# Inverting the triangular blocks of a delta-rule kernel on lanes of 16x16 instead of 32x32, in all twelve groups

## The chip, the cores and the metric

The kernel runs on one core of one Trainium2 chip. The time is the device time of one execution in microseconds. Before the change it is 664.31 us, the median of 3 runs (662.4 to 664.77).

## The reference

Two layers follow each other. The first is a delta-rule attention over 4 batches, 8 heads, 768 positions and a head size of 48; the second is a gated MLP on its output.

```python
k_n = k / (np.linalg.norm(k, axis=-1, keepdims=True) + 1e-06)
for t in range(S):
    y[:, :, t] = np.einsum('bhd,bhde->bhe', q[:, :, t], state)
    v_old = np.einsum('bhde,bhd->bhe', state, kt)
    state = state + bt * np.einsum('bhd,bhe->bhde', kt, vt - v_old)
# x: y with the heads side by side, (4, 768, 384)
h = np.maximum(x @ w_in, 0.0)                 # 1024 wide
u, v = h[..., :512], h[..., 512:]
v_n = (v - mean(v)) / sqrt(var(v) + 1e-06)    # over the 512
v_s = einsum('ts,bsd->btd', w_spatial, v_n) + b_spatial[None, :, None]
out = (u * v_s) @ w_out
```

## The kernel before

**The recurrence in chunks.** Each batch's 768 positions are cut into 12 chunks of 64 (`CH`). One *step* handles one chunk of one batch for all 8 heads: 4 pairs of heads (`NU`) in the free dimension, and the two heads of a pair on partitions 0 to 63 and 64 to 127. There are 48 steps. `ORDER` runs them as two chains of two batches each: six steps of the first chain alone, then one of each chain in turn, and six of the second chain alone.

Within a chunk the recurrence needs the inverse of a triangular 64x64 matrix per head, made of products of the keys (`products`, which multiplies on TensorE at line 359 and masks the results into the tile `ta` on VectorE). Four steps form a *group* (`G = 4`), and there are 12 groups; the blocks of a group are inverted together.

**Lanes.** The small triangular blocks on the diagonal are inverted by substitution on VectorE, each partition (a *lane*) working on its own block, so that one instruction handles all blocks of a group. To spread the blocks over lanes, `bounce` (line 399) writes the group's products to a buffer in DRAM, and loads pick the blocks out of it.

- Groups 1 to 11 use lanes of 32x32: `load_la` loads the block's rows in two parts with eight DMAs (line 512), `load_wt` and `load_wb` copy them into a work tile on ScalarE (lines 522 and 529), and `lanes` does 30 rounds of a multiply (line 543) and an add (line 550) on VectorE. A group has 64 such blocks; each is split over two lanes, its even rows on one and its odd rows on the other. The result goes to DRAM (`wd`, line 559, two DMAs) and comes back into `ta` (line 564, four DMAs).
- Group 0 uses lanes of 16x16, one block to a lane, 128 blocks: `load16` takes four DMAs (line 422), `copy16` one ScalarE copy, and `lanes16` does 14 rounds (lines 441 and 448). The inverted 16x16 blocks are stored (four DMAs, line 453), and `ta` is read back whole (line 458). Then two blocks of 16 are widened to one of 32 on TensorE: per step one VectorE transpose (line 465), 16 products (line 474), one ScalarE copy that masks half the rows (line 481), 16 more products (line 487) and four ScalarE copies into `ta` (line 493). `C16` is the number of steps that share one PSUM tile of the pool `pa`, one mask copy and one set of four copies; it is 1. On the chip one such product in 32-bit floats is two matmul instructions.

Both ways end with blocks of 32. The widening from 32 to 64 is part of every step: `step_t` transposes on VectorE (line 575), `step_e` and `step_f` multiply on TensorE (585, 597) and copy on ScalarE (588, 600). A step then has `step_a` (642, with an add on VectorE at 645), `step_b` (659, scaled at 663), `step_c` (678, added to the state at 682) and `step_d` (692, copied out at 703). All of these take their PSUM tiles from the pool `pa`, four banks in turn.

**The MLP.** When four chunks of a batch are done, `convert` splits the result into two parts for exact products, and tasks are put in a list: `mlp_v` (line 759), `mlp_u` (820), `mlp_g` (839) and `mlp_o` (884). They are TensorE work between the recurrence's pieces: `fill(rate)` emits a given amount of it after each part of a step, and what is left follows after the last step. The weights come in 64-bit floats and are decoded by short VectorE and ScalarE operations (line 156 and 183) in the first third.

**The order.** The prologue (all up to the loop over steps) sets VectorE's order by hand: group 0's lanes, with pieces of group 1's lanes (`X1 = 14` of them, and `M4` later) and of the weights' conversion between. In the loop a planner orders every engine's instructions by a simulated time and by priority: the parts of a step have a higher one (`hp`), products, lanes and MLP have that of their place. The lanes of group g+2 begin to be emitted in the third step of group g (`if sl == LS`), a few pieces at a time (`lane(n)` advances the oldest generator in `lq` by n pieces); before the fourth step of group g ends, the code makes sure that group g+1's lanes are emitted. `W16 = 16` is a number of empty pieces between the store of the 16x16 blocks and the first transpose, for groups other than 0. All loads and stores are issued by SP, in order.

The few lines that choose between the two ways:

```python
if g + 2 < G16:
    load16(g + 2)
    copy16(g + 2)
    lq.append(lanes16(g + 2))
else:
    load_la(g + 2)
    load_wt(g + 2)
    lq.append(lanes(g + 2))
```

Of the kernel before, what the change touches and what calls it, by code (L numbers as in the profile page):

```python
# [7 lines left out]
F32 = mybir.dt.float32  # L8
# [11 lines left out]
G = 4  # L20
# [8 lines left out]
R0 = 1.5  # L29
TD = 1  # L30
TP = 4
G16 = 1
C16 = 1
W16 = 16
X1 = 14
R1 = 1.7
# [42 lines left out]
def delta_rule_gated_mlp(  # L79
# [14 lines left out]
    nc = tc.nc  # L94
    PSUM = bass.MemoryType.PSUM
    const = ctx.enter_context(tc.tile_pool(name="const", bufs=1))
    grp = ctx.enter_context(tc.tile_pool(name="grp", bufs=2))
# [144 lines left out]
    def pump1():  # L242
        n = count["dve"]
        for _ in range(3 * len(tasks)):
            if not tasks or count["dve"] > n:
                break
            t = tasks.pop(0)
            if t[1] > 0:
                t[1] -= 1
            else:  # L250
                try:
                    t[1] = next(t[0])
                except StopIteration:
                    continue
            tasks.append(t)
# [139 lines left out]
    def bounce(g):  # L395
        ad_g[g] = dram.tile([CH, 2, G * NU, CH], F32, name="ad")
        ta = ta_g[g][:, 0].rearrange("p s u t -> p (s u) t")
        for h in range(2):
            mark["ad"] = nc.sync.dma_start(out=ad_g[g][:, h], in_=ta[rows_t(h)])

    ws = [const.tile([128, 16, 32], F32, name=f"w{i}") for i in range(2)]
    for w in ws:
        nc.gpsimd.memset(w[:, 8:16, 0:16], 0.0)

    def lane_map(g, blk):
        p0, r0 = blk * 32, blk * 16
        src = ad_g[g].rearrange("j h n t -> (h n) j t")
        return slice(p0, p0 + 32), src[:, r0 : r0 + 16, r0 : r0 + 16]

    buf16 = {}  # L410

    def load16(g):
        if g < 2:
            t = moe.tile([128, 512], F32, name="la16", tag="vl", bufs=VB)
        else:
            t = grp.tile([128, 16, 32], F32, name="la", bufs=1).rearrange("p j t -> p (j t)")
        buf16[g] = t
        la = t[:, 0:256].rearrange("p (j t) -> p j t", t=16)
        w = t[:, 256:512].rearrange("p (j t) -> p j t", t=16)
        for blk in range(4):  # L420
            pr, sq = lane_map(g, blk)
            mark["la"] = nc.sync.dma_start(out=la[pr], in_=sq)
        w_g[g] = [la, w]
# [5 lines left out]
    def lanes16(g):  # L429
        la, w = w_g[g]  # L430
# [29 lines left out]
        for _ in range(W16 if g else 0):  # L460
            yield
        pp = px = None
        for s in range(G):
            tr = buf16[g][:, s % 2 * 256 : s % 2 * 256 + 256].rearrange("p (u t) -> p u t", t=CH)
            t_ins = nc.vector.transpose(out=tr.rearrange("p u t -> p (u t)"), in_=ta[:, s].rearrange("p u t -> p (u t)"))
            yield
            if s % C16 == 0:
                pp = pa.tile([128, 512], F32, name="pa")
                px = pp[:, 256:512].rearrange("p (s u t) -> p s u t", u=NU, t=16)
                pp = pp[:, 0:256].rearrange("p (s u t) -> p s u t", u=NU, t=16)  # L470
            for u in range(NU):
                for q in range(4):
                    r, c = q * 32, q % 2 * 32
                    nc.tensor.matmul(
                        pp[r : r + 32, s, u], ta[r : r + 16, s, u, c : c + 32], tr[r : r + 16, u, c : c + 16],
                        start=True, stop=True,
                    )
            if s % C16 < C16 - 1:
                continue
            ss = slice(s - C16 + 1, s + 1)  # L480
            nc.scalar.mul(out=pi[:, ss], in_=pp[:, ss], mul=hm)
            yield
            for z in range(s - C16 + 1, s + 1):
                for u in range(NU):
                    for q in range(4):
                        r, c = q * 32, q % 2 * 32
                        p_ins = nc.tensor.matmul(
                            px[r : r + 16, z, u], pi[r : r + 32, z, u], ta[r : r + 32, z, u, c + 16 : c + 32],
                            start=True, stop=True,
                        )  # L490
            for q in range(4):
                r, c = q * 32, q % 2 * 32
                nc.scalar.copy(out=ta[r : r + 16, ss, :, c + 16 : c + 32], in_=px[r : r + 16, ss])
            if s == C16 - 1:
                mark["t16"], mark["p16"] = t_ins, p_ins
            yield s
# [76 lines left out]
    def step_t(s):  # L573
        tn_t[s] = work.tile([128, NU, 32], F32, name="tn", bufs=1)
        nc.vector.transpose(out=tn_t[s], in_=t_of(s)[:, :, 0:32])

    def step_e(s):
        tt, tn = t_of(s), tn_t.pop(s)
        pi = pi_t[s] = work.tile([128, NU, 32], F32, name="pi", bufs=1)
        p2 = pa.tile([128, 512], F32, name="pa")  # L580
        pp = p2[:, : NU * 32].rearrange("p (u c) -> p u c", c=32)
        for u in range(NU):
            for h in range(2):
                r, lo = slice(h * 64, h * 64 + 32), slice(h * 64 + 32, h * 64 + 64)
                nc.tensor.matmul(pp[lo, u], tt[r, u, 32:64], tn[r, u, :], start=True, stop=True)
        for h in range(2):
            lo = slice(h * 64 + 32, h * 64 + 64)
            nc.scalar.copy(out=pi[lo], in_=pp[lo])
# [361 lines left out]
    def urgent():  # L950
        return tc.high_priority(offset=5000)

    def after(*names):
        es = ExitStack()
        for n in names:
            es.enter_context(tc.issue_after(mark[n].ins))
        return es

    with tc.manual_schedule(engines={ET.DVE}):
# [45 lines left out]
        def kk_outs(g):  # L1005
            for t in range(g * G, g * G + G):
                mask_c(t)
                part_out(t, 0)
            bounce(g)
            if g < G16:  # L1010
                load16(g)
                copy16(g)
            else:
                load_la(g)
                load_wt(g)
# [19 lines left out]
        mcs.pop()  # L1035
        l0, l1 = lanes16(0), (lanes16 if G16 > 1 else lanes)(1)
        with after("la"):
# [7 lines left out]
        def run(gen, end, every):  # L1045
            n = 0
            for y in gen:
                if y == end:
                    return
                n += 1  # L1050
                if every and n % every == 0:
                    pump1()
# [5 lines left out]
        with urgent():  # L1058
            if G16 > 1:
                pass  # L1060
# [4 lines left out]
        for k in range(M5):  # L1065
            pump1()
        with urgent():
            run(l0, 0 if C16 == 1 else G - 1, 0)
            step_t(0)
            step_e(0)  # L1070
            step_v(0)
# [6 lines left out]
    for s in range(NST + 1):  # L1078
        g, sl = divmod(s, G)
# [14 lines left out]
        def slot_a():  # L1094
# [10 lines left out]
            if sl == LS and g + 2 < NG:  # L1105
                if g + 2 < G16:
                    load16(g + 2)
# [160 lines left out]
```

## Time and profile before

| | |
|---|---|
| median of 3 runs | 664.31 us |
| profiled execution's span | 665.8 us |
| TensorE matmul busy | 564.1 us, 85% |
| VectorE busy | 449.3 us, 67% |
| ScalarE busy | 264.3 us, 40% |
| GpSimd busy | 205.0 us, 31% |
| mean granted TensorE clock | 0.885 |

The profiled execution is not among the three timed runs; its own time is known by its span, 665.8 us, from the first to the last instruction.

A row of a group of instructions reads: line, engine, operation, output<-input with shapes, count | busy us, mean ns of one | idle time of the engine just before them, and what ended it. Busy time is time in which the engine had at least one such instruction in flight; matmuls overlap, so a mean of 212 ns does not say that the next one starts 212 ns later. Rows of a stretch of time give each engine's busy time with the number of instructions in brackets, then the granted TensorE clock as a share of full speed, the DMA engines' busy share and GB/s. PE is TensorE's matmul, PEld its weight load, DVE is VectorE, ACT is ScalarE, POOL is GpSimd, SPq is the queue from which SP issues DMAs.

### The profile page before, as it was taken

How to read it: one execution, taken by the hardware profiler on the slowest of the kernel's cores; microseconds unless marked ns; L12 is line 12 of the kernel's file. 1: busy time of each engine (PE TensorE's matmuls, PEld its weight loads, DVE VectorE, ACT ScalarE, POOL GpSimd, SP SyncE). 2: the span in 40 equal slices, each digit the busy share in tenths (PEclk: the TensorE clock that was granted, in tenths of full speed). 3: DMA queues.
4: the chain of work that ended last, by engine and by line, in shares of the span. 5: the costliest groups of instructions: out<-in, count | busy, mean ns of one | idle time of the engine just before them, and what ended most of it. 6: DMA issues, size and time to landing. Idle time of an engine off the chain costs nothing.

```text
span 665.8 us, 19042 instructions
## 1 busy us (share of the span) xinstructions
PE 564.1 (85%) x7432; PEld 490.7 (74%) x7432; DVE 449.3 (67%) x1565; ACT 264.3 (40%) x712; POOL 205.0 (31%) x250
## 2 busy tenths in 40 slices
PE   5425758758759797999999899989999999999997
PEld 4324647647648576888878778879898789998997
DVE  3588968999879768788595685799836822223142
ACT  1223233552437254432432646731326574215321
POOL 4114445463324324133322224233213133310000
PEclk9998656955588787889899899998999899999999
DMA  8554386847553563724537436454253231101001
GB/s 235 132 127 131 106 178 202 232 115 186 146 108 109 151 140 89 158 86 112 109 107 187 93 100 172 97 130 94 78 130 84 71 69 42 46 19 36 1 25 48
DMA packets 144522, 74.63 MB, mean 112 GB/s; under 512 B 105136, under 2 KB 128432, under 8 KB 144432
## 3 DMA queue, kind: packets, MB, share of 16 engines
q1 hardware_dynamic: 144432, 73.41, 43.6%
q8 instruction: 59, 0.97, 0.6%
q14 instruction: 31, 0.25, 0.1%
HBM read 58.16 MB, written 14.02 MB: 108 GB/s over the span
## 4 chain that ended last, share of the span: by engine, by line
PE 44%; DVE 13%; DMA 7%; SPq 5%; issue 2%; ACT 2%; POOL 0%; DVEq 0%; ACTq 0%
PE pm L839 11%; PE pm L820 6%; PE pm L884 4%; DVE prod L543 4%; PE pm L759 4%; DVE w L550 4%; PE pa L692 2%; PE pa L659 2%; PE pa L642 2%; PE pq L359 2%; PE pa L678 2%; PE pma L839 2%; DMA kqa<-in_qa_t 2%; PE pa L597 2%; PE pma L884 1%
## 5 line engine op out<-in xcount | busy, mean ns | idle before, releaser
L550 DVE TENSOR_TENSOR w<-w,prod 128x30 f32<-128x30 f32 (+4 forms) x330 | 102.1, 309 | 9.0 <-issue 2.2
L839 PE MATMUL pm<-wsp_h,vh 128*128 128x256 f32 x252 | 74.6, 296 | 0.0
L839 PE MATMUL pm<-wsp_h,vl 128*128 128x256 f32 x252 | 74.6, 296 | 0.0
L359 PE MATMUL pq<-kq 128*64 128x128 f32 x640 | 63.1, 320 | 13.2 <-DVE ta L156 7.6
L839 PE MATMUL pm<-wsp_l,vh 128*128 128x256 f32 x252 | 74.3, 295 | 0.0
L543 DVE TENSOR_TENSOR prod<-w,la 128x30 f32<-128x30 f32 (+8 forms) x180 | 62.6, 348 | 13.0 <-ACT w L522 8.7
L659 PE MATMUL pa<-v,ta 64*64 64x48 f32 x768 | 46.2, 249 | 26.4 <-DVE v L645 12.0
L659 PEld LDWEIGHTS pa<-v,ta 64*64 64x64 f32 x768 | 37.0, 159 | 38.6 <-ACT ta L600 10.9
L359 PEld LDWEIGHTS pq<-kq 128*64 128x64 f32 x640 | 45.5, 160 | 22.7 <-issue 8.5
L628 POOL TENSOR_TENSOR v<-v,cn 128x192 f32<-128x192 f32 x48 | 24.7, 515 | 118.1 <-DMA v<-in_kv_nat 83.4
L543 DVE TENSOR_TENSOR prod<-w,lb 128x120 f32<-128x120 f32 (+3 forms) x150 | 54.4, 363 | 3.8
L839 PEld LDWEIGHTS pm<-wsp_h,vh 128*128 128x128 f32 x252 | 50.0, 199 | 1.4 <-issue 0.7
L600 ACT COPY ta<-pa 32x128 f32<-32x128 f32 x96 | 24.3, 253 | 67.0 <-PE pa L597 65.7
L839 PEld LDWEIGHTS pm<-wsp_h,vl 128*128 128x128 f32 x252 | 49.8, 198 | 1.4 <-issue 0.7
L642 PE MATMUL pa<-su,kqa 48*64 48x48 f32 x704 | 39.2, 239 | 13.6 <-DMA kqa<-in_qa_t 6.6
L839 PEld LDWEIGHTS pm<-wsp_l,vh 128*128 128x128 f32 x252 | 49.9, 198 | 0.9 <-issue 0.2
L663 DVE TENSOR_TENSOR su<-pa,cn 64x192 f32<-64x192 f32 x96 | 33.8, 352 | 22.5 <-PE pa L659 21.3
L341 POOL TENSOR_TENSOR mc<-mpos,cn 128x256 f32<-128x256 f32 x44 | 27.0, 615 | 67.8 <-DVE ta L156 58.3
L642 PEld LDWEIGHTS pa<-su,kqa 48*64 48x64 f32 x704 | 30.9, 149 | 22.2 <-issue 12.8
L682 DVE TENSOR_TENSOR su<-su,pa 48x192 f32<-48x192 f32 x88 | 31.0, 352 | 20.0 <-PE pa L678 18.1
L692 PE MATMUL pa<-kqa,su 128*64 128x64 f32 (+1 forms) x768 | 44.4, 250 | 0.0
L678 PE MATMUL pa<-su,knat 64*48 64x48 f32 x704 | 35.3, 227 | 5.8 <-DVE su L663 5.6
(144 smaller groups left out, 1294.8 us busy)
## 6 DMA issues: line engine op xcount, KB each, us to landing
kq<-in_kp_t SPq DMA_DIRECT2D x40, 384.0 KB, 3.9
ad<-ta SPq DMA_DIRECT2D x24, 256.0 KB, 3.9
kqa<-in_qb_t SPq DMA_DIRECT2D x48, 128.0 KB, 2.7
kqa<-in_qa_t SPq DMA_DIRECT2D x48, 96.0 KB, 2.6
v<-in_kv_nat SPq DMA_DIRECT2D x48, 96.0 KB, 2.3
knat<-in_kv_nat SPq DMA_DIRECT2D x48, 96.0 KB, 2.3
out<-ob SPq DMA_DIRECT2D x24, 192.0 KB, 2.0
kn<-in_kv_nat SPq DMA_DIRECT2D x20, 192.0 KB, 3.4
```

The source lines that it names most:

```text
L359: nc.tensor.matmul(p1[rows_t(h), u], kq[:, h, u, :], kq[:, h : 3 : 2 - h, u, :], start=True, stop=True,)
L543: (nc.gpsimd if PG0 <= g < PG1 else nc.vector).tensor_tensor(out=pr, in0=w[:, :n, j : j + 1].broadcast_to([128, n, m]), in1=(la[:, j, j + ...
L550: nc.vector.tensor_add(out=w[:, :n, j + 1 : 32], in0=w[:, :n, j + 1 : 32], in1=pr)
L642: nc.tensor.matmul(pr[rows_t(h), u], kqa[rows_d(h), 1, u, :], su_view(su, h, u, rows_d(h)), start=True, stop=True)
L659: mark["pb"] = nc.tensor.matmul(pu[rows_t(h), u], tt[rows_t(h), u, :], r[rows_t(h), u, :], start=True, stop=True)
L663: mark["db"] = nc.vector.tensor_tensor(out=su_all(su, h, rows_t(h)), in0=pu[rows_t(h)], in1=cn[rows_t(h), 1].unsqueeze(2).broadcast_to([64 ...
L678: nc.tensor.matmul(ps[rows_d(h), u], kn[rows_t(h), u, :], su_view(su, h, u, rows_t(h)), start=True, stop=True)
L682: nc.vector.tensor_add(out=su_all(nx, h, rows_d(h)), in0=su_all(su, h, rows_d(h)), in1=ps[rows_d(h)])
L692: nc.tensor.matmul(py[rows_t(h), u], su_view(su, h, u, kr, 64), kqa[kr, 2 - 2 * h, u, :], start=True, stop=True)
L820: nc.tensor.matmul(pu[:, k], w[:, kt, d0 : d0 + 128], a[:, kt], start=(n == 0), stop=(n == 3 * NK - 1))
L839: nc.tensor.matmul(p[:, k], v[i][:, d0 : d0 + 128], w[:, si, ts], start=(n == 0), stop=(n == 3 * NT - 1))
L884: nc.tensor.matmul(po[:, :DM], a[:, d, ts], w[:, d], start=(n == 0), stop=(n == 3 * ND - 1))
```

## The change

All twelve groups use lanes of 16x16 (`G16 = 12`). In groups 1 to 11 a whole group shares one PSUM tile in the widening (`c16(g)` is 1 for group 0 and 4 for the others), so a group has one mask copy and four ScalarE copies of four times the size, beside four transposes and 2x64 products. The two constant work tiles of the 32x32 lanes, `ws`, and their clearing are gone; the tile that holds a group's blocks and work area has two buffers from group 2 on, where it had one. The functions `load_la`, `load_wt`, `load_wb` and `lanes` stay in the file and are no longer called. In the prologue group 1 is loaded by `load16` and `copy16`, and the hand-set pieces of group 1's lanes are pieces of `lanes16`.

```diff
-G16 = 1
-C16 = 1
+G16 = 12
 W16 = 16
...
-    ws = [const.tile([128, 16, 32], F32, name=f"w{i}") for i in range(2)]
-    for w in ws:
-        nc.gpsimd.memset(w[:, 8:16, 0:16], 0.0)
-
...
+    def c16(g):
+        return 1 if g == 0 else G
+
     def load16(g):
         if g < 2:
             t = moe.tile([128, 512], F32, name="la16", tag="vl", bufs=VB)
         else:
-            t = grp.tile([128, 16, 32], F32, name="la", bufs=1).rearrange("p j t -> p (j t)")
+            t = grp.tile([128, 512], F32, name="la", bufs=2)
...
         for _ in range(W16 if g else 0):
             yield
         pp = px = None
+        C16 = c16(g)
         for s in range(G):
...
         with urgent():
-            run(l0, 0 if C16 == 1 else G - 1, 0)
+            run(l0, 0, 0)
             step_t(0)
```

## The prediction

> **What bounds the kernel now.** I read the page's busy rows first, then its strips of 40 slices, then the busy time cut at the steps, then the waits.
>
> ```profile
> span 665.8 us, 19042 instructions
> PE 564.1 (85%) x7432; PEld 490.7 (74%) x7432; DVE 449.3 (67%) x1565; ACT 264.3 (40%) x712; POOL 205.0 (31%) x250
> DVE  3588968999879768788595685799836822223142
> PEclk9998656955588787889899899998999899999999
> ```
>
> The span is 1.5 us above the median of the three runs (664.31). I sum against the span and take 1.5 off at the end. VectorE is at 0.8 to 0.99 in the first third and TensorE's clock is low there (0.5 to 0.8); later the clock is full and VectorE falls. So I cut the span at the transposes that open a step (`step_t`): group 1 begins at 96.1, group 2 at 153.3, then 193.4, 240.0, 281.7 (group 5); the last recurrence matmuls are at 591.
>
> ```profile
> core 0: us, PE busy (x) PEld busy (x) DVE busy (x) ACT busy (x) POOL busy (x), PEclk, DMA share, GB/s
> 44.60:96.00 51.40, 30.84 (x590) 25.55 (x592) 42.68 (x145) 16.33 (x56) 21.41 (x30) 0.70 0.51 128
> 96.00:153.30 57.30, 40.98 (x549) 34.37 (x546) 52.78 (x170) 26.25 (x68) 30.76 (x32) 0.68 0.66 173
> 153.30:193.40 40.10, 32.30 (x434) 26.55 (x430) 34.62 (x128) 13.01 (x39) 13.02 (x18) 0.61 0.57 147
> 193.40:240.00 46.60, 36.36 (x534) 30.64 (x534) 37.77 (x141) 22.91 (x64) 19.09 (x25) 0.78 0.53 135
> 240.00:281.70 41.70, 37.52 (x503) 31.53 (x504) 33.11 (x134) 21.13 (x60) 11.40 (x14) 0.84 0.54 131
> 281.70:591.00 309.30, 299.04 (x4013) 258.92 (x4013) 201.16 (x698) 132.56 (x355) 96.36 (x98) 0.97 0.40 98
> ```
>
> Three stages follow. Early (44.6 to 281.7, 237.1 us, 20 steps): VectorE 42.68+52.78+34.62+37.77+33.11 = 201.0 us, 85%; TensorE's busy time times its clock is 129 us, so half of what it could do. Late (281.7 to 591): TensorE 299.04 of 309.3, idle 10.3. Tail (591 to 665.8): the MLP's remainder, which the change leaves as it is. VectorE matters early, TensorE late.
>
> What holds a step back is seen at the group borders.
>
> ```profile
> DVE tn L575 <- DMA ta<-wd: 11.0, 7, 4.1
> ...
> 69.02 0.25 DVE L575 STREAM_TRANSPOSE tn<-ta 128x128 f32<-128x128 f32 x1
> 96.10 0.29 DVE L575 STREAM_TRANSPOSE tn<-ta 128x128 f32<-128x128 f32 x1
> ...
> 202.08 0.30 DVE L575 STREAM_TRANSPOSE tn<-ta 128x128 f32<-128x128 f32 x1
> 217.80 0.31 DVE L575 STREAM_TRANSPOSE tn<-ta 128x128 f32<-128x128 f32 x1
> 230.80 0.18 DVE L550 TENSOR_TENSOR w<-w,prod 128x15 f32<-128x15 f32 x1
> 240.00 0.31 DVE L575 STREAM_TRANSPOSE tn<-ta 128x128 f32<-128x128 f32 x1 [0.56 <-DMA ta<-wd]
> ...
> 232.75 1.37 SPq L559 DMA_DIRECT2D wd<-w  x2
> ```
>
> Inside group 3 two steps take 217.80-202.08 = 15.7 us, 7.9 each. The next step, the first of group 4, comes 22 us later: group 4's last lane operation ends at 231, its store is issued at 232.75, and the transpose starts the moment the loaded block lands. Seven of the twelve groups begin in a wait for that load. Group 1 waits too: 27 us between step 3 and step 4. The early pace is 237.1/20 = 11.9 us a step. So the lanes, not the recurrence, set the pace early, and late they run beside a full TensorE.
>
> **The change part by part.**
>
> *Lanes of 32 taken off VectorE.*
>
> ```profile
> L550 DVE TENSOR_TENSOR w<-w,prod 128x30 f32<-128x30 f32 (+4 forms) x330 | 102.1, 309 | 9.0 <-issue 2.2
> L543 DVE TENSOR_TENSOR prod<-w,la 128x30 f32<-128x30 f32 (+8 forms) x180 | 62.6, 348 | 13.0 <-ACT w L522 8.7
> L543 DVE TENSOR_TENSOR prod<-w,lb 128x120 f32<-128x120 f32 (+3 forms) x150 | 54.4, 363 | 3.8
> ...
> 44.60:281.70 237.10, 53.47 (x146) 0.72 0.56 144
> 44.60:281.70 237.10, 46.18 (x145) 0.72 0.56 144
> ```
>
> 660 operations, 219.1 us, 19.9 us a group. The last two rows are lines 543 and 550 in the early stage alone: 99.7 us, 291 operations of 60 a group, 4.85 groups. Some of it is no work of theirs:
>
> ```profile
> 180.56 1.80 POOL L737 TENSOR_TENSOR xl<-xs,xh 128x768 fp32r<-128x768 f32 x1
> 180.64 1.80 DVE L543 TENSOR_TENSOR prod<-w,lb 128x56 f32<-128x56 f32 x1
> 182.47 0.22 DVE L550 TENSOR_TENSOR w<-w,prod 128x56 f32<-128x56 f32 x1
> ```
>
> The same 56 elements take 0.22 us alone and 1.80 while GpSimd works on SBUF. The mean of all 660 is 332 ns, about 1.35 times the 0.25 us that I estimate for them undisturbed.
>
> *Lanes of 16 put on VectorE.* Group 0 shows them:
>
> ```profile
> L441 DVE TENSOR_TENSOR prod<-la x14: 161/204/216, 23.3 to 34.1; 128x14 f32<-128x14 f32 x2, 128x26 f32<-128x26 f32 x2, 128x36 f32<-128x36 f32 x2, 128x44 f32<-128x44 f32 x2
> L448 DVE TENSOR_TENSOR la<-la,prod x14: 173/203/217, 23.5 to 34.3; 128x14 f32<-128x14 f32 x2, 128x26 f32<-128x26 f32 x2, 128x36 f32<-128x36 f32 x2, 128x44 f32<-128x44 f32 x2
> L465 DVE STREAM_TRANSPOSE la<-ta 128x256 f32<-128x256 f32 x4 | 1.6, 428 | 1.8 <-DMA kqa<-in_qa_t 1.8
> L474 PE MATMUL pa<-la,ta 16*32 16x16 f32 x128 | 2.9, 212 | 18.7 <-DVE la L465 18.7
> L487 PE MATMUL pa<-ta,prod 32*16 32x16 f32 x128 | 1.8, 185 | 1.1 <-ACT prod L481 1.1
> L493 ACT COPY ta<-pa 16x64 f32<-16x64 f32 x16 | 3.2, 203 | 1.8 <-PE pa L487 0.9 <-PE pa L474 0.7
> ```
>
> 28 operations of 0.204 are 5.7 us, 7.7 with the same factor of 1.35; four transposes 1.6; a memset 0.07: 9.4 us a group for 19.9. Early that takes 99.7-4.85*9.4 = 54 us from VectorE, leaving 147 of 237; over the kernel 11*10.5 = 116, leaving about 333.
>
> *Widening put on TensorE.* Group 0 shows 2.9+1.8 = 4.7 us for its 256 small instructions; eleven more groups, 52 us. Early, 4.85*4.7 = 23 us go on 129: 152 of 237, into idle time, and a denser TensorE may hold a higher clock. Late are groups 6 to 11, 6*4.7 = 28 us, where only 10.3 us are idle: **+18 us**. Ends: -10 (all 28 between the pipelined matmuls, and the idle gone as well, since VectorE falls from 201 to about 140 there) and +28 (none hidden). I take 28 less the 10.3 idle.
>
> The rows price these instructions at 14 (line 487) to 23 ns (line 474). By the Trainium skill, "TensorE: Matmul & The Clock Gate", Part 1, starts are never closer than about 25 ns: 256*25 = 6.4 us a group as an estimate, late 38 for 28, and the forecast would be 10 us higher. Line 487's 14 ns disagrees, so the rows stand.
>
> *ScalarE and queues.* A group loses four copies (lines 522 and 529) and gains six: into `w`, the scaled one, and four of line 493's kind with four times its 64 columns. Were each three times 203 ns and nothing taken off, that is 3.7 us a group, on an engine that is busy for 40% of the span: I take nothing, covered by its idle time; without the cover it is 11*3.7 = 40 us at most, were all of it on the path. DMAs: 14 a group (four `la`, four `lb`, two `wd`, four back) become 10 (four, four, two). SP issues fewer, and each still stands behind the same kind of wait (lanes done, store landed). What waits behind the widening: the transposes stand in VectorE's order behind the load back, the matmuls in TensorE's order behind transpose and ScalarE copy. With twelve blocks early enough this costs nothing; else see the second rival. In the prologue SP issues four loads for group 1 instead of eight, before step 0's loads:
>
> ```profile
> 27.83 4.05 SPq L512 DMA_DIRECT2D la<-ad  x8
> 33.43 0.17 DVE L448 TENSOR_TENSOR la<-la,prod 128x36 f32<-128x36 f32 x1 [4.69 <-issue]
> ```
>
> Half of 4.05 is **-2 us**; ends 0 and -4.7, VectorE's gap.
>
> *What the freed VectorE time is worth early.* Group 1's lanes end some 10 us sooner (32 operations fewer of 332 ns), and no later group waits for its blocks. The floor is 152 us (TensorE at full clock), VectorE's is 147, and 20 steps at the ungated 7.9 us are 158. Next in line are the prefetch waits and the weights' conversion on VectorE, which stay. I take the middle between 7.9 and 11.9, 9.9 us a step, 198 us: **-39**. Ends: -79 (7.9 throughout) and -11 (only the seven waits go).
>
> Sum: -39-2+18 = -23; 665.8-23 = 642.8, less 1.5: **641 us**, with 622 to 658 as this case's own range.
>
> **The rivals.**
> 1. *The early gain is full.* All early steps at 7.9: -79-2+18 = -63, 601 us. For it: three limits near 150 us. Against it: they would have to overlap perfectly at a clock of 0.6 to 0.8. 0.12.
> 2. *Waits in order replace the gate.* The transposes of line 465 stand at the head of VectorE while the block's load is under way, and a whole group holds one of four `pa` banks until its last copy. A wait as long as the longest at line 575 (about 4 us) in the 4.85 early groups is 19 us: 660. Against it: 16 empty turns lie between store and transposes. 0.10.
> 3. *TensorE pays it back.* Something else early, such as the weights' conversion, holds the steps, so only the waits go (-11), and late nothing is hidden (+28): -11-2+28 = +15, 679, slower. It decides when the early gain is below 26 us. 0.14.
> 4. *The small matmuls mix with others.* When 32-row tiles alternate with larger ones they get slow:
>
> ```profile
> 282.73 0.24 PE L585 MATMUL pa<-tn,ta 32*32 32x32 f32 x2
> ...
> 285.80 0.31 PE L642 MATMUL pa<-su,kqa 48*64 48x48 f32 x2
> ...
> 354.16 0.67 PE L642 MATMUL pa<-su,kqa 48*64 48x48 f32 x16
> 354.76 0.44 PE L597 MATMUL pa<-ta,pi 32*32 32x32 f32 x16
> ```
>
> Sixteen pairs in turn took 3.4 us (282.73 to 286.1); the same numbers in two blocks 1.1. That is 2.3 us for 32 instructions, 18 us for a group's 256, 111 late. A fifth of them mixed eats the 23 us; two fifths give 641+44 = 685, slower. Against it: the two rows of 16, and group 0, ran in blocks. 0.14. The Trainium skill, "TensorEngine Tiling (Array Packing)", Key Properties, says that a change of tiling mode drains the array, and the alternating rows agree; it speaks against this change, which puts 22 more batches of small tiles between full-size matmuls.
>
> **How the numbers follow.** The forecast has 0.50. Faster by over 0.5% (about what a measurement here can tell from no change: below 661): 0.50+0.12 and over half of rival 2, 0.68. Within 0.5%: the rest of rival 2 and the low edge of 4, 0.06. Slower: rivals 3 and 4, 0.26. The range 612 to 680 takes in the forecast's own, rivals 2 and 3 and part of 4; the rest of 1 and 4 is left out.
>
> **What would show it.** Right: lines 543, 550, 559 and 564 gone; lines 441 and 448 with 168 operations each; lines 474 and 487 with 1536 each, in blocks; VectorE near 333 us; TensorE's busy time up by 30 to 50; step 4's transpose before 85 instead of 96.1; group 5's near 240 instead of 281.7; no transpose waiting for a group's load; last recurrence matmul near 568. Wrong: group 5 beginning after 265; line 474 or 487 in pairs between lines 839 or 820; long waits at line 465; a late stage over 335 us.

## The result: 15% slower

The changed kernel takes 768.33 us (median of 4, 761.68 to 775.73), the kernel before beside it 664.54: a ratio of 1.1521, 95% interval 1.1462 to 1.158. The forecast was 641 with a range to 680, so both the sign and the range were wrong. The profiled execution is the longest of the four (span 773.5 us; the others 759 to 767): the ratio leaves it out, and stage times read from it are up to 2% high.

The head of the page after, with the strips of VectorE and of TensorE's clock:

```profile
span 773.5 us, 24364 instructions
PE 632.1 (82%) x10248; PEld 555.2 (72%) x10248; DVE 355.2 (46%) x1246; ACT 273.5 (35%) x734; POOL 201.4 (26%) x248
DVE  4756885966353643535333725451234432312242
PEclk9995558655785587896699979876989889999999
```

VectorE is relieved as meant, mostly 0.2 to 0.5 after the first third. But the clock falls to 0.6 and 0.7 in the second half of the span too, where before it wasn't under 0.8. The new operations, from the groups of instructions after:

```profile
L439 DVE TENSOR_TENSOR prod<-la 128x14 f32<-128x14 f32 (+6 forms) x168 | 44.8, 267 | 40.1 <-ACT la L425 36.5
L446 DVE TENSOR_TENSOR la<-la,prod 128x14 f32<-128x14 f32 (+6 forms) x168 | 45.2, 269 | 3.9
L464 DVE STREAM_TRANSPOSE la<-ta 128x256 f32<-128x256 f32 x48 | 19.1, 424 | 64.9 <-DMA ta<-ad 60.5 <-PE pa L473 4.3
L473 PE MATMUL pa<-la,ta 16*32 16x16 f32 x1536 | 34.2, 195 | 41.5 <-DVE la L464 40.7 <-issue 0.9
L486 PE MATMUL pa<-ta,lb 32*16 32x16 f32 x1280 | 18.7, 180 | 2.3 <-issue 2.2
L486 PE MATMUL pa<-ta,prod 32*16 32x16 f32 x256 | 3.8, 187 | 1.4 <-issue 0.9 <-ACT prod L480 0.5
```

(Line numbers of the new file are smaller by one here.) All prices were met: the lanes take 90.0 us for twelve groups, 7.5 each (forecast 7.7), the transposes 1.6 a group, and the products 34.2+18.7+3.8 = 56.7, less group 0's 4.7 the 52 us of the forecast. What these operations cost the kernel was wrong.

I cut both spans at the transpose of line 575 (574 after) that opens group 5 and at the end of the last recurrence matmul: early, late and tail, first before, then after. Columns are as in the prediction.

```profile
44.60:281.70 237.10, 177.99 (x2597) 148.63 (x2598) 200.97 (x713) 99.62 (x286) 95.68 (x119) 0.72 0.56 144
281.70:592.10 310.40, 300.14 (x4029) 259.76 (x4029) 201.16 (x698) 132.56 (x355) 96.44 (x98) 0.97 0.40 97
592.10:665.80 73.70, 69.62 (x489) 67.21 (x488) 22.94 (x60) 24.53 (x52) 1.85 (x1) 1.00 0.08 29
```

```profile
47.20:312.10 264.90, 198.62 (x3796) 167.78 (x3797) 158.94 (x556) 100.88 (x291) 92.49 (x118) 0.67 0.47 127
312.10:699.90 387.80, 347.51 (x5646) 305.21 (x5644) 148.79 (x538) 141.45 (x376) 96.33 (x99) 0.87 0.30 78
699.90:773.50 73.60, 69.59 (x488) 67.19 (x488) 22.96 (x60) 24.54 (x52) 1.84 (x1) 1.00 0.08 29
```

The 107.7 us more are +2.6 in the prologue, +27.8 early, +77.4 late and -0.1 in the tail. The forecast had -2, -39, +18 and 0. Late, TensorE is busy for 47 us more, idle for 40.3 instead of 10.3, and its clock is 0.87 instead of 0.97. The stage has 5646 matmuls for 4029: the 1536 small products of groups 6 to 11, and 81 others that before ran in the early stage.

The waits after show what is new at the widening:

```profile
DVE la L464 <- DMA ta<-ad: 60.5, 13, 8.1
PE pa L473 <- DVE la L464: 40.7, 9, 20.6
PE pa L641 <- DMA kqa<-in_qa_t: 21.4, 7, 7.7
```

VectorE stands 60.5 us at the transposes for a group's load, as the second rival said, but VectorE has time now. Of the 40.7 us of the second row some 19 were there before, in group 0. The third is a load of the recurrence, 6.6 us before.

The theories I tested: **waits** (the widening sits in the engines' order with its PSUM bank, and the recurrence stands behind it), **TensorE's work** (the products cost by themselves, by their time or by their kind), **the clock** (TensorE at half clock for lack of full-size work), and **the planner's order** (a tuned order is upset). The table has the stages of each kernel by the same cuts, in us, the clock granted in the late stage where I use it, and the ratio to the kernel before (664.5 us beside the changed one, 667 to 668 beside the others):

```
kernel       prologue  early   late   tail  late clock  median   ratio [95%]
before           44.6  237.1  310.4   73.7     0.97     664.5
after            47.2  264.9  387.8   73.6     0.87     768.3    1.152 [1.146, 1.158]
x_hp             46.3  257.6  397.6   73.6              775.9    1.160 [1.151, 1.169]
x_bank           45.8  250.2  394.4   81.3              773.7    1.152 [1.139, 1.165]
x_step           46.9  251.4  389.6   65.8              763.9    1.140 [1.128, 1.153]
x_kqa3           48.5  255.7  401.8   73.6              777.4    1.163 [1.157, 1.170]
x_nowiden        46.5  221.4  333.4   89.3     0.90     693.3    1.031 [1.017, 1.045]
x_nolanes        45.1  212.2  338.4   89.4     0.92     683.4    1.026 [1.019, 1.033]
x_g2             47.9  244.9  311.7   81.3     0.96     687.9    1.031 [1.024, 1.038]
x_pework         47.8  246.4  395.8   76.7     0.85     768.4    1.150 [1.143, 1.157]
x_pehalf         46.0  248.1  352.2   74.1     0.89     716.2    1.073 [1.062, 1.084]
x_peearly        46.0  248.9  359.1   73.7     0.90     721.9    1.082 [1.073, 1.092]
x_pelate         45.6  235.9  386.1   76.7     0.84     745.7    1.115 [1.110, 1.119]
x_bigwork        46.2  233.8  347.3   73.7     0.98     702.8    1.045 [1.031, 1.059]
x_perows         45.6  266.3  414.1   81.5     0.80     811.8    1.216 [1.211, 1.221]
x_fill           50.8  227.7  310.4   81.4     0.97     673.9    1.007 [1.003, 1.011]
x_fillhalf       47.4  223.3  313.7   81.4     0.95     666.1    0.998 [0.994, 1.002]
x_nl3            46.0  237.3  301.7   81.4              668.1    1.001 [0.997, 1.006]
x_x1             45.9  241.0  306.2   73.7              669.5    1.003 [0.998, 1.007]
x_warm           48.4  270.6  402.3   75.1     0.91     796.4    (too scattered)
```

### The profile page after: what moved, and what is told of

Same layout as the page of the kernel before. It is cut to its first block, busy times and chain, and to the rows that moved or that the text cites. A ratio compares the mean times of both kernels' runs of the same rounds, so it can differ in the third digit from the quotient of the medians.

```text
span 773.5 us, 24364 instructions
## 1 busy us (share of the span) xinstructions
PE 632.1 (82%) x10248; PEld 555.2 (72%) x10248; DVE 355.2 (46%) x1246; ACT 273.5 (35%) x734; POOL 201.4 (26%) x248
## 4 chain that ended last, share of the span: by engine, by line
PE 46%; DMA 22%; DVE 14%; SPq 9%; issue 4%; ACT 3%; POOL 1%; DVEq 0%; ACTq 0%; POOLq 0%
PE pm L838 10%; PE pm L819 4%; PE pa L691 4%; DMA ad<-ta 4%; DMA ta<-ad 4%; PE pm L883 4%; DMA ad<-la 4%; PE pa L658 3%; DVE prod L439 3%; DVE la L446 3%; PE pq L358 3%; PE pa L677 3%; PE pa L641 3%; DMA la<-ad 3%; DMA kn<-in_kv_nat 3%
## 5 line engine op out<-in xcount | busy, mean ns | idle before, releaser
L358 PE MATMUL pq<-kq 128*64 128x128 f32 x640 | 66.7, 345 | 2.8 <-DVE ta L155 2.7
L473 PE MATMUL pa<-la,ta 16*32 16x16 f32 x1536 | 34.2, 195 | 41.5 <-DVE la L464 40.7
L641 PE MATMUL pa<-su,kqa 48*64 48x48 f32 x704 | 41.1, 250 | 30.2 <-DMA kqa<-in_qa_t 21.4
L439 DVE TENSOR_TENSOR prod<-la 128x14 f32<-128x14 f32 (+6 forms) x168 | 44.8, 267 | 40.1 <-ACT la L425 36.5
L473 PEld LDWEIGHTS pa<-la,ta 16*32 16x32 f32 x1536 | 26.2, 120 | 49.6 <-issue 37.2
L641 PEld LDWEIGHTS pa<-su,kqa 48*64 48x64 f32 x704 | 33.1, 160 | 37.8 <-issue 22.2
L358 PEld LDWEIGHTS pq<-kq 128*64 128x64 f32 x640 | 50.6, 175 | 10.6 <-issue 4.8
L662 DVE TENSOR_TENSOR su<-pa,cn 64x192 f32<-64x192 f32 x96 | 34.0, 354 | 48.7 <-PE pa L658 47.8
L691 PE MATMUL pa<-kqa,su 128*64 128x64 f32 (+1 forms) x768 | 50.1, 272 | 4.9 <-DVE v L644 4.9
L677 PE MATMUL pa<-su,knat 64*48 64x48 f32 x704 | 38.8, 241 | 13.5 <-DVE su L662 13.5
L464 DVE STREAM_TRANSPOSE la<-ta 128x256 f32<-128x256 f32 x48 | 19.1, 424 | 64.9 <-DMA ta<-ad 60.5
L446 DVE TENSOR_TENSOR la<-la,prod 128x14 f32<-128x14 f32 (+6 forms) x168 | 45.2, 269 | 3.9
```

What stands on the lines that cost most here:

```text
L358: nc.tensor.matmul(p1[rows_t(h), u], kq[:, h, u, :], kq[:, h : 3 : 2 - h, u, :], start=True, stop=True,)
L439: nc.vector.tensor_tensor(out=pr, in0=w[:, :j, j : j + 1].broadcast_to([128, j, m]), in1=la[:, j, j + 1 : 16].unsqueeze(1).broadcast_to([1 ...
L446: nc.vector.tensor_add(out=w[:, :j, j + 1 : 16], in0=w[:, :j, j + 1 : 16], in1=pr)
L473: nc.tensor.matmul(pp[r : r + 32, s, u], ta[r : r + 16, s, u, c : c + 32], tr[r : r + 16, u, c : c + 16], start=True, stop=True,)
L641: nc.tensor.matmul(pr[rows_t(h), u], kqa[rows_d(h), 1, u, :], su_view(su, h, u, rows_d(h)), start=True, stop=True)
L662: mark["db"] = nc.vector.tensor_tensor(out=su_all(su, h, rows_t(h)), in0=pu[rows_t(h)], in1=cn[rows_t(h), 1].unsqueeze(2).broadcast_to([64 ...
```

## The experiments

**Is it the wait at the widening?** `x_hp` lets the widening's instructions go ahead of up to 1000 that stand before them in the planner's order, `x_step` shares nothing between the steps of a group, `x_bank` gives the widening a PSUM bank of its own, out of `pa`'s four. All start from the changed kernel.

```diff
-            t_ins = nc.vector.transpose(out=tr.rearrange("p u t -> p (u t)"), in_=ta[:, s].rearrange("p u t -> p (u t)"))
+            with tc.high_priority(offset=1000):
+                t_ins = nc.vector.transpose(out=tr.rearrange("p u t -> p (u t)"), in_=ta[:, s].rearrange("p u t -> p (u t)"))
...
+                    with tc.high_priority(offset=1000):
+                        nc.tensor.matmul(
```

> The changed kernel with every instruction of the widening (transposes, both sets of products, mask copy, copies) given priority over what is emitted up to 1000 instructions before it; nothing else differs. Theory A (the widening is small work that stands behind less urgent work in the planned order, and the step that opens a group waits for its last copy): from the landing of the block to the last copy falls from about 30 us to about 10 in a group, and the time from 768 to 650-700. Theory B (the work of the small matmuls on TensorE, with the drains between tile sizes, is the cost): 755-775, no matter where they stand. Theory C (VectorE standing at the transposes until the load back has landed, 60.5 us in the changed kernel): 765-790, since the transposes then stand even earlier in VectorE's order.

```diff
     def c16(g):
-        return 1 if g == 0 else G
+        return 1
```

> The changed kernel with the widening done a step at a time in all groups (one PSUM tile, mask copy and four copies for each step, as in group 0), not a group at once. Theory A: the step that opens a group needs only its own quarter, so the wait shortens by more than half: 690-735, in spite of 12 more ScalarE copies a group. Theory B: same matmuls, 760-775. Theory D (a group's widening holds one of the four PSUM banks of the recurrence for tens of us, which stops the steps): 690-735 too, and then a bank of its own must show it.

```diff
-NPA=4
+NPA=3
...
+    pw = ctx.enter_context(tc.tile_pool(name="pw", bufs=1, space=PSUM))
...
-                pp = pa.tile([128, 512], F32, name="pa")
+                pp = pw.tile([128, 512], F32, name="pp16") if g else pa.tile([128, 512], F32, name="pa")
```

> The changed kernel with a PSUM bank of its own for the widening of groups 1 to 11; the recurrence has three banks in turn instead of four. Theory D (the widening holds one of the recurrence's four banks for tens of us and stops its steps): 690-735. Theory E: 755-785, nothing gained, some lost by the fourth bank.

None gains more than a per cent: 775.9, 763.9 and 773.7. `x_hp` did move the widening: from a group's first transpose to its last small product it takes 12 us (median of groups 1 to 11) where the change takes 34, and that product ends 19 us before the group's first step, where in the change it is 1.6. So in the change the widening is the last thing that most groups wait for, and yet the time is no shorter without that wait. Neither the widening's rank in the order nor the bank it holds is the cause. (`x_bank` also takes a bank from the recurrence; early it is 15 us faster than the change, late 7 slower.)

**Each half alone.** `x_nowiden` keeps the lanes of 16 and leaves the widening out; `x_nolanes` takes two of 30 rounds of the 32x32 lanes in groups 2 to 11 and adds nothing; `x_pework` is the kernel before with the widening's 128 products a group added on a constant tile, with nobody waiting for them.

```diff
-        for s in range(G):
+        for s in range(G if g == 0 else 0):
```

> The changed kernel with the widening from 16 to 32 left out in groups 1 to 11 (no transposes, no small products, no copies; the blocks between stay as they are, so the result is not the attention): the lanes of 16, their store and their load back stay. Gives what the lanes alone are worth. Theory A and B alike below before: 600-640. If it stays above 700, neither holds and the loss lies in the lanes' loads and stores.

```diff
-        for j in range(1, 31):
+        for j in range(1, 31) if g == 1 else (1, 8):
```

> The kernel before with nearly all of the substitution left out in groups 2 to 11 (2 of its 30 rounds stay; the loads, copies, stores and loads back stay), so that the result is not the attention: some 170 us less on VectorE and nothing added anywhere. The prediction's step (early, VectorE's lanes set the pace; freeing them is worth about 39 us and more when nothing is added): 600-630. Theory F (the freed VectorE time is worth little, the steps are held by something else): 650-690.

```diff
+        yield
+        dm = pa.tile([128, 512], F32, name="pa")
+        for z in range(8):
+            for u in range(NU):
+                for q in range(4):
+                    r, o = q * 32, z % 4 * 64 + u * 16
+                    if z < 4:
+                        nc.tensor.matmul(
+                            dm[r : r + 32, o : o + 16], mpos[r : r + 16, 0:32], mpos[r : r + 16, 0:16],
...
+                    else:
+                        nc.tensor.matmul(
+                            dm[r : r + 16, 256 + o : 256 + o + 16], mpos[r : r + 32, 0:16], mpos[r : r + 32, 16:32],
...
+            yield
```

> The kernel before, with 128 small products of the widening's shapes added in each of groups 1 to 11, on a constant tile, into a PSUM tile that nobody reads: the same TensorE work, with nobody waiting for it. Theory A: it fills idle time early and costs some 18 to 28 us late: 675-700. Theory B: it costs most of the 104 us: 730-770.

The products alone make the whole loss: 768.4 us for the change's 768.3, at the prices expected (groups of instructions of `x_pework`):

```profile
L574 PE MATMUL pa<-mpos 16*32 16x16 f32 x1408 | 29.0, 190 | 0.1
L579 PE MATMUL pa<-mpos 32*16 32x16 f32 x1408 | 25.2, 183 | 3.4 <-issue 3.4
```

54.2 us of small products cost 101 (768.4 less the 667 to 668 of the kernel before beside it). That the two agree so closely is partly chance, as the other half alone has a price, too: a VectorE freed by itself gains nothing, and both other kernels are about 3% slower than before. The stages of `x_nolanes` and, below them, the matmuls of the MLP's line 820 in its early stage and in that of before:

```profile
45.10:257.30 212.20, 157.01 (x2418) 131.88 (x2418) 131.40 (x455) 90.00 (x261) 89.59 (x114) 0.69 0.61 148
257.30:595.70 338.40, 323.39 (x4087) 271.86 (x4087) 108.24 (x394) 139.43 (x375) 92.31 (x98) 0.92 0.39 96
595.70:685.10 89.40, 85.31 (x608) 82.89 (x608) 24.33 (x62) 26.97 (x57) 8.91 (x7) 0.99 0.08 29
...
45.10:257.30 212.20, 17.37 (x108) 15.35 (x108) 0.69 0.61 148
```

```profile
44.60:281.70 237.10, 22.93 (x144) 20.60 (x144) 0.72 0.56 144
```

The early steps do come faster: 212.2 us instead of 237.1. But TensorE does 21 us less in them (157.01 busy, 177.99 before), 36 matmuls of line 820 fewer among others; that work comes back later. The tail has 608 matmuls instead of 489 and is 15.7 us longer, the late stage 28. Of these 44 us some 20 are the work put off, taken at full clock (178.0*0.72 less 157.0*0.69); the rest is TensorE late at a clock of 0.92 for 0.97 and idle for 15 us for 10. Busy time times clock over the three stages is 157.0*0.69+323.4*0.92+85.3*0.99 = 490, against 178.0*0.72+300.1*0.97+69.6 = 489 before: the same work for TensorE, put off.

**How much, and where.** `x_pehalf` adds half of the small products (`for z in (0, 1, 4, 5)`), `x_peearly` all of them but in groups 1 to 5 alone, `x_pelate` in 6 to 11 alone; `x_g2` makes the change for group 1 alone.

```diff
+        if g >= 6:
+            return
```

> The kernel before with 64 instead of 128 small products added in each of groups 1 to 11, on a constant tile. Theory E, and any theory by amount of work: 705-725, half of the 101 us. Theory D (holding one of four PSUM banks, whatever is done with it): 750-770, since a bank is still taken once a group.

> The kernel before with the 128 small products a group, read by nobody, added in groups 1 to 5 alone. The prediction's step (early they fall into TensorE's idle time): 664-675. If small products cost the same everywhere: 668+101*5/11 = 714.

> The same in groups 6 to 11 alone. The prediction's step (28 us of work, 10.3 of it in idle time): 686. If small products cost the same everywhere: 668+101*6/11 = 723.

```diff
-G16 = 1
-C16 = 1
+G16 = 2
...
```

> The kernel before with the change made for group 1 alone (a group at once), groups 2 to 11 with lanes of 32. The first theory of the prediction (the lanes of group 1 hold step 4 back): step 4's transpose at 85 instead of 96, time 650-660. Theory E: the one group's small products fall where the clock is at half anyway, 664 with step 4 little earlier: 660-672.

Half costs 48, near half of 101, so there is no threshold. The two parts cost +54 and +78, together more than the whole, and each more than both forecasts of it. The early and the late stage of `x_pelate`:

```profile
45.60:281.50 235.90, 177.70 (x2597) 148.69 (x2597) 200.83 (x713) 99.73 (x286) 96.26 (x119) 0.71 0.57 145
281.50:667.60 386.10, 341.96 (x5541) 296.92 (x5540) 204.22 (x698) 132.84 (x354) 94.42 (x97) 0.84 0.33 79
```

Up to group 5 it is the kernel before to a microsecond. Then the products, 28.4 us of busy time in six groups, make the late stage 75.7 longer: 41.8 in busy time at a clock of 0.84 instead of 0.97, and 33.9 in idle time. That is the change's late loss (77.4), alone. `x_peearly` loses its time elsewhere than where its products are: 11.8 us early, 48.7 in the late stage, where only 102 of its 1280 instructions run (2 us). A stretch of that stage, with the group of before that answers to it (group 7) below, and TensorE's instructions in it:

```profile
338.00:420.00 82.00, 82.00 (x660) 62.47 (x660) 32.82 (x108) 14.18 (x39) 16.35 (x18) 0.73 0.29 73
```

```profile
364.00:412.00 48.00, 45.70 (x581) 38.04 (x580) 32.66 (x127) 27.31 (x70) 16.41 (x18) 0.96 0.47 112
```

```profile
384.30 0.31 PE L604 MATMUL pa<-tn,ta 32*32 32x32 f32 x2
384.55 0.58 PE L858 MATMUL pm<-wsp_h,vh 128*128 128x256 f32 x1
385.06 0.31 PE L604 MATMUL pa<-tn,ta 32*32 32x32 f32 x2
385.30 0.58 PE L858 MATMUL pm<-wsp_l,vh 128*128 128x256 f32 x1
385.81 0.31 PE L604 MATMUL pa<-tn,ta 32*32 32x32 f32 x2
```

In group 7 the order has the recurrence's products (lines 585, 597 and 678 of before) in turn with single matmuls of the MLP, 0.75 us a turn, without a gap, at half clock. TensorE is busy for all of the 82 us, with 660 matmuls where before there are 581 in 48. Stretches with one or two instructions to a line, six or more of them in a row, take about 7 us before, 34 in `x_peearly` and `x_nolanes`, 45 in `x_nowiden`, 8 in `x_pework` and 16 after. So this mixing is a part of the loss where work has been moved, and not what makes the products dear.

The new products don't run in blocks either. In `x_pework` other matmuls break them into 271 pieces, 170 of them of four instructions or fewer; in the change it is 270 and 177. Nearly nine of ten neighbours of a piece are the recurrence's, only 32 of 512 in the change the MLP's. The number of pieces doesn't carry the price: with 64 products a group, 183 pieces cost 48 us (`x_pehalf`) and 114 pieces 144 (`x_perows`, below). No run here has the small products in unbroken blocks, so a part for the breaking up isn't excluded.

`x_g2` pays 3% for one group, more than either forecast: 3 us in the prologue, 8 early and 8 in the tail; one group's products are 5 us.

**Is it TensorE's time, or the kind of work?** `x_bigwork` puts 44 full-size matmuls (of type fp32r, as the MLP's) at the place of the products, `x_perows` puts 64 products with as few columns but on 128 rows and 64 columns of the array, the shape of line 692; `x_warm` adds the full-size ones to the change.

```diff
+        for z in range(8):
+            for _ in range(5 + z % 2):
+                nc.tensor.matmul(dm[:, 0:256], big[:, 0:128], big[:, 0:256], start=True, stop=True)
+            yield
```

> The kernel before with 44 full-size matmuls (128x128 weights, 256 columns, about 0.12 us each: 5.3 us) added in each of groups 1 to 11, at the same places and into the same kind of PSUM tile as the 128 small products were, which nobody reads. Theory E (what costs is that TensorE works on small tiles or waits in more of the time, and then its clock is granted at half: 138 us of full-speed time lost to the clock in the changed kernel, 77 before): full-size work holds the clock, so 680-720, with a mean clock at or above 0.87. Theory B' (any 5 us of TensorE time a group costs 9 us, by the planned order or the PSUM bank): 755-780, as with the small products.

```diff
+                    r, o = q % 2 * 64, z * 64 + u * 16
+                    nc.tensor.matmul(
+                        dm[r : r + 64, o : o + 16], mpos[:, 0:64], mpos[:, q * 16 : q * 16 + 16],
...
```

> The kernel before with 64 products a group added in groups 1 to 11, as many as in the run with half of the small products (716), but each on 128 rows and 64 columns of the array, the shape of the recurrence's last matmuls, instead of 16 or 32 rows. Nothing waits for them. Small products cost 1.8 us for each us that they hold TensorE, full-size ones 0.6. If it is the small tile (the array's switch of shape, or the clock that small tiles do not hold) that makes the price, these cost 0.6 to 0.9 of their own TensorE time (4 to 7 us a group, my estimate), 25 to 55 us less than 1.8 of it: about 695 to 715. If short instructions of any shape cost that much at this place, 1.8 of it: 745 or more.

> The changed kernel with 44 full-size matmuls of about 0.12 us (5.3 us a group, 58 in all) added behind each widening of groups 1 to 11, into a PSUM tile that nobody reads. Theory E (time is lost because little of TensorE's work is full-size and its clock stays at half): the added work comes nearly free, 760-790, with a mean clock of 0.86 or more in place of 0.82. Theory B' (TensorE time costs as such): 768+35 = 800 or more, as the same work cost in the kernel before.

TensorE's busy rows of `x_bigwork` and of `x_pework`, then the late stage of `x_bigwork`, and the row of the new products and the late stage of `x_perows`:

```profile
PE 614.2 (88%) x7916; PEld 543.8 (78%) x7916; DVE 447.0 (64%) x1565; ACT 266.0 (38%) x714; POOL 203.2 (29%) x250
...
280.00:627.30 347.30, 335.69 (x4363) 297.01 (x4361) 205.61 (x731) 138.51 (x371) 97.15 (x100) 0.98 0.37 90
```

```profile
PE 615.0 (80%) x10248; PEld 541.0 (71%) x10248; DVE 456.5 (60%) x1565; ACT 265.4 (35%) x712; POOL 206.6 (27%) x250
```

```profile
L573 PE MATMUL pa<-mpos 128*64 128x16 f32 x1408 | 78.9, 240 | 0.0
...
311.80:726.00 414.20, 376.89 (x4879) 332.47 (x4880) 211.61 (x730) 137.19 (x368) 94.06 (x99) 0.80 0.32 77
```

Both `x_bigwork` and `x_pework` make TensorE busy for 50 us more (564.1 before), and the one costs 35 us, the other 101. Full-size work costs 37 late, where it keeps the clock at 0.98, and nothing early. Against the busy time of their own rows, the full-size matmuls cost 0.4 of it (35 for 79.5), the short products of the large shape 1.8 (144 for 78.9) and the small ones 1.9 (101 for 54.2). So a high price doesn't need a tile of 16 or 32 rows. Against the rise of TensorE's whole busy time it is 0.7, 1.3 (144 for 107) and 2.0, so that a part for the small tile isn't excluded. What both short kinds have in common is 16 columns to a weight load, but also their type: they are 32-bit floats, two instructions to a product. No run here tells the two apart.

`x_warm` scattered too much for a ratio: 780.96, 796.39 and 798.0, at mean clocks of 0.89, 0.86 and 0.86 (0.82 to 0.84 in the change). The first fits theory E, the others lie between the two. Full-size work beside the small products raises the clock, then, but doesn't win their loss back.

**Is it the clock?** `x_fill` puts full-size matmuls, read by nobody, where `fill` finds no MLP task in the first 16 steps (the order came to have 423 of them, not the 230 expected), `x_fillhalf` half as many.

```diff
+                    if not tail[0] and nxt["s"] < 16 and pend["pm"] < 2:
+                        dm = pm.tile([128, 512], F32, name="pm")
+                        for _ in range(int(1.0 * bank["c"] / 0.109)):
+                            nc.tensor.matmul(dm[:, 0:256], big[:, 0:128], big[:, 0:256], start=True, stop=True)
...
```

> The kernel before with full-size matmuls on a constant tile (128x128 weights, 256 columns, read by nobody) where the first 16 steps find no MLP work to emit, as many as the missing work would have had: about 230 of 0.12 us. Theory E (early, TensorE's clock is at half because little of its work is full-size; with it the steps' matmuls would run at full clock): group 5 begins before 275 instead of 282 and the time is 645-665. Otherwise the added work is in the way: 670-700.

> The same with half as many matmuls. Theory E: between, 650-668. Otherwise 668-685.

The early stage of `x_fillhalf`:

```profile
47.40:270.70 223.30, 177.36 (x2666) 149.67 (x2665) 195.30 (x699) 94.26 (x274) 95.67 (x115) 0.78 0.60 151
```

The early clock rises from 0.72 to 0.78 (0.82 in `x_fill`) and the stage is 14 us shorter (9). The prologue is 3 (6) longer, the late stage 3 (0) and the tail 8, and nothing is left: 0.998 and 1.007. But of the kernel's own matmuls the early stage has 56 (86) fewer and the tail 65 (64) more, and the added ones take time too. So no gain was had this way, and what a higher clock early is worth by itself these runs don't show.

**Is it the order, or a buffer?** `x_nl3` and `x_x1` change two numbers that the planner's order hangs on (`NL = 4` to 3, `X1 = 14` to 10). `x_kqa3` is the change with a third buffer for the tile whose load TensorE waits for in the third row of waits above.

> The kernel before with three instead of four pieces of the lanes emitted at each place (NL = 3): the same instructions, in another planned order (about an eighth of TensorE's order differs). Shows what another order alone costs. Theory G (the kernel before stands at a tuned order, and any other loses 20 us or more, as the change for group 1 alone did): 680-695. Otherwise: 660-672.

> The kernel before with 10 instead of 14 pieces of group 1's lanes in the first gap of the prologue (X1 = 10): the same instructions, another order from the prologue on. Theory G: 680-695. Otherwise: 662-675.

```diff
-            kqa = kqa_t[s] = work.tile([128, 3, NU, CH], F32, name="kqa", bufs=2)
+            kqa = kqa_t[s] = work.tile([128, 3, NU, CH], F32, name="kqa", bufs=3)
```

> The changed kernel with three buffers instead of two for the tile `kqa`, whose load the recurrence's matmuls wait for (21.4 us in the changed kernel, 37.3 in the one with small products added, 6.6 before). If these loads, late by their buffer, are what turns small products into idle time of TensorE, the row goes and the time falls by its 15 to 20 us, to about 750. If the loads are only the place where a recurrence that is slowed elsewhere comes to stand, the time stays within 1% of the changed kernel's 768 and the idle time shows up at another tile.

These two other orders cost nothing (1.001 and 1.003). With the third buffer TensorE waits 3.7 us for the tile instead of 21.4, and the time doesn't fall (777.4, 1.2% above the change and so a little outside what was expected):

```profile
  DMA kqa<-in_qa_t: 3.7, 3
```

So that wait was only a place where a slower recurrence came to stand.

## Why the prediction was wrong, step by step

- *What bounds the kernel.* "VectorE matters early, TensorE late" held, but I took the stages as independent. TensorE's work is the same in sum, and what isn't done early is done later.
- *Lanes of 32 off VectorE, lanes of 16 on:* right. The summed durations of VectorE's operations fall by 113.5 us, 507.2 to 393.6, for the 116 forecast. Its busy time falls by 94 only, to 355 instead of 333, because operations overlap and the sum isn't the busy time; I had taken the one from the other.
- *Widening put on TensorE, +18:* this step failed. The instruction time was right (52 us), its worth was not. Early it was to vanish in idle time; late it was to cost 28 less 10 of idle time. Alone and needed by nobody, it costs 101 us in all and 76 late (`x_pework`, `x_pelate`). My upper end, "none hidden", +28, was no upper end: late each us of these products costs 2.7 (75.7 for 28.4). Nor did it use the idle time, which grew from 10.3 to 40.3 us.
- *The clock:* "a denser TensorE may hold a higher clock" was wrong in sign. Full-size matmuls raised the mean from 0.885 to 0.924 (`x_bigwork`); short ones lowered it to 0.824 (small) and 0.787 (large shape).
- *What the freed VectorE time is worth early, -39:* this step failed, too. `x_nolanes` shows -25 early, better than my lower end of -11, and +44 behind it, late and tail together. With the lanes alone (`x_nowiden`) it is -16, and step 4 begins at 85.3, as forecast. In the change even that isn't there: step 4 begins at 95 (96.1 before), after group 1's last small product at 90.6, and group 5 at 312.
- *ScalarE and queues at nothing:* not contradicted; ScalarE is busy 9 us more. *Prologue -2:* it became +2.6.
- *The rivals.* The first (full gain) fell. The second's waits are there, 60.5 us of them, but rank, bank and grouping changed at will bring no gain, so they carry no price that shows. The third (TensorE pays it back) was nearest: right in sign and in both conditions, an early gain below 26 and nothing hidden late; its 679 had the late price at 28 for 77 and an early gain of 11 for a loss of 28. The fourth named mixing with other matmuls. It happens: between the recurrence and the MLP where work has moved, and between the new products and the recurrence, which break each other into small pieces. But the new products' rows keep their 52 us, so the price isn't where that rival put it, in their own time.

**What stays open.** Of the change's late 77 us, busy time at a lower clock makes 47 and idle time 30. Most falls of the clock have idle time before them: 20 of 25 in the change come after a stretch of 3.41 us (the unit of the trace's clock record) in which TensorE was busy for under 0.8. In `x_pework`'s late stage it falls 7 times, each time after one with TensorE busy for 0.70 or less; the kernel before has 5 falls there. What grows more is how long the clock stays down: 35 of 116 such stretches are at half clock, 6 of 91 before. Why the recurrence leaves TensorE idle more often beside short products, no run here shows: in the stage where they run, idle time and half clock rise together, and beside full-size ones neither does. Nor do the stages add: the early loss of 28 has -16 from the lanes alone (`x_nowiden`) and +12 from the products alone (`x_peearly`), and the rest only comes with both.

None of these kernels beats the one before.

## What to carry to other kernels

Price work that goes to an engine by the stage where that engine is full, and by the kind of work: here short matmuls cost 1.8 to 2.7 times the busy time of their rows and full-size ones 0.4 to 0.9 (35 us for 79.5 in all, 37 for 39.4 late). A stage that ends sooner has gained only if the engine that bounds the next one has done as much by then: compare its busy time times its clock, not the steps' pace. And try the added operations alone first, in the old kernel with nobody waiting for them: one such run would have shown the loss here.

## What was not expected of the hardware

A TensorE that never pauses can stay at half clock. Five microseconds out of 35 of that kind in `x_peearly` (375 to 410 us):

```profile
385.00:390.00 5.00, 5.00 (x27) 4.08 (x28) 0.00 (x0) 0.51 (x2) 0.00 (x0) 0.50 0.00 0
```

TensorE is busy for all of the 5 us, with full-size matmuls between recurrence products, and the granted clock is 0.50. By the Trainium skill, "TensorE: Matmul & The Clock Gate", Part 1, the gate opens after a window of about 3.4 us of sustained activity and closes after an idle one. That isn't what this row shows: busy in the profile's sense wasn't enough for 35 us, and with short products in the late stage (`x_pelate`, busy for 341.96 of 386.10) the clock was 0.84.

What sorts the clock here is the number of columns that TensorE streams (256 for a 128x256 matmul, 16 for a new product). I cut the traces into the clock record's stretches of 3.41 us and add up the columns of the matmuls that start in each. In the kernel before, 33 stretches at half clock had under 3100 columns, and the clock opened after none of them; 12 had more, and it opened after all. At full clock 12 had fewer, and it fell after all; 121 had more, and it fell after one. In `x_pework` it is none of 49 and 18 of 30 at half, 18 of 20 and 1 of 107 at full. Busy time sorts the falls as well (12 of 13 before and all 19 in `x_pework` follow a stretch with TensorE busy for under 0.8), but not the openings: of the stretches at half clock with TensorE busy for 0.95 or more, 12 of 20 were followed by full clock before and 17 of 36 in `x_pework`. In `x_peearly` around the row above, nine of eleven stretches at half clock had 1344 to 2560 columns. So short products can keep TensorE busy without opening the clock. The bound is fitted to these traces, and no run changed the columns alone.
